# Twelve tiles of the imaginary hidden DFT move from the front of a DFT-attention kernel into its short attention sections, and most output projections move to the end

## The chip, the core and the metric

The kernel runs on one core of one Trainium2 chip. The metric is the device time of one execution in microseconds. A core has five engines with their own instruction streams: TensorE (PE), VectorE (DVE), ScalarE (ACT), GpSimd (POOL) and SyncE (SP, which here only issues DMAs). They are ordered against each other by semaphores alone.

## What is computed

For a sequence of 2048 tokens of width 512, a gate mixes two branches of the same input:

```
g = sigmoid((x * gate_w).sum(-1, keepdims=True))
a = x @ dft_hid_re.T ;  b = x @ dft_hid_im.T          # DFT along the hidden dimension
y = dft_seq_re @ a - dft_seq_im @ b                   # DFT along the sequence, real part
q, k, v = split_heads(x @ wqkv, 32 heads of 16)
o = softmax(q @ k.T * 16 ** -0.5) @ v                 # per head, then heads joined
out = g * y + (1 - g) * (o @ wo)
```

## The kernel before

**Precision.** Every float32 operand of the dense products is split into a high and a low fp32r part, and each product of two operands becomes three TensorE products (high-high, high-low, low-high). With four blocks of 128 along the hidden dimension, one 128x512 tile of `x @ W` takes 12 products of 512 columns. The value products of the attention are plain float32 (two TensorE instructions each).

**Front.** The q and k projections come first, then V (16 tiles of 12 products) and the imaginary hidden DFT `b` (16 tiles of 12). The first 8 V tiles are made with all 128 rows of the array. The other 8 and all 16 tiles of `b` go through `pairs_of` and `phase`: every product is cut into two row halves of 64, and two tiles run beside each other, one in each half. A phase has 24 such half products, and four phases make four tiles. Into them go the first score tiles for the row maxima (`a_tile`: one 128x512 score tile, reduced to its maxima by DVE, L296), `LEAD` = 57 key blocks for two heads each: alternately six and four tiles a phase. A tile of `b` is copied out of PSUM by ACT, split by POOL, and stored to DRAM (`b_done`, L370 to L373); for the first four tiles `b_done` also splits one block of the real DFT weight into SBUF (`wre`).

**Attention sections.** From then on TensorE works in sections that one string of slots each writes out by hand. A section belongs to one row half: the dense products of the DFT chain go into that half and score products into the other one, beside them. In a string, `a` is a score tile for a maximum (ended by a DVE reduce, 683 ns), `s` a score tile for an exponential (ended by an ACT activation, 628 ns); the digit is the PSUM bank; `-` is a dense product alone; a slot of two letters has no dense product but one score tile in each half; `|` are the value products of one unit. A unit is one key tile of one pair of heads for half of the queries: four exponentials fill its `pt` tile, then four value products add into the bank `acc`. Each section holds two units. Bank 6 is `acc` itself: between the copy that empties it at a section's start (`part`, ACT, L832) and the value products at the section's end it serves as a seventh bank for scores. Two sections, one for each half, make one chain of dense products.

There are three kinds. 13 pairs of short sections (THIN) hold the real hidden DFT, 12 products to a chain; ACT copies the finished tile out as `y` (L492) and POOL splits it back into `xab`. 96 pairs of FULL sections hold the sequence DFT, 16 products. 13 pairs of NINE sections hold output projections without their last block of heads, 9 products; their strings have the two units' value products apart. All maxima and exponentials come from two streams that the strings consume in order, so a string's letters also set which unit's exponentials are how far ahead of its value products.

**Tail.** The last 22 units have no maxima left. Scores, value products and the rest of the projections are interleaved by a loop over units (`sides`, `whole`), then the last head pair is finished (`LastPair`). SP's DMAs are issued in the order of the program, many of them by a table of due units (`at`, `run_plan`).

What orders the engines around a section's end: the first value product of a section overwrites `acc`, so it waits for the exponential that still reads a score in bank 6; and a unit's last value product waits for the last of the four exponentials that fill its `pt`.

Of the kernel before, what the change touches and what calls it, by code (L numbers as in the profile page):

```python
# [15 lines left out]
P = 128  # L16
# [8 lines left out]
LEAD = 57  # L25
# [6 lines left out]
def mix_kernel(ctx: ExitStack, tc: tile.TileContext, xa_t, xa, wqkv, w_hid, w_seq, wo, gate_w, out):  # L32
# [52 lines left out]
    oh_d = [[dram.tile([P, 2, S // 2], F32, name=f"oh{hf}{ct}") for ct in range(3)] for hf in range(2)]  # L85
# [29 lines left out]
    wv = [[const.tile([P, D], F32R, name=f"wv{v}{kt}", tag=f"w{4 * v + kt}") for kt in range(KT)] for v in range(2)]  # L115
    wch = st1.tile([P, KT, D], F32R, name="wch")
    wcl = st1.tile([P, KT, D], F32R, name="wcl")
# [77 lines left out]
    with tc.tile_pool(name="qk", bufs=1, reuse_waits="tile") as pool:  # L195
# [24 lines left out]
        for kt in range(KT):  # L220
            add(wch[:, kt], wcl[:, kt], w_hid[1, :, kt], nc.gpsimd)
# [145 lines left out]
    def b_done(s, ps):  # L367
# [6 lines left out]
        if s < KT:  # L374
            hi_lo(wre[0][s], wre[1][s], wrs.pop(0), nc.gpsimd)
# [42 lines left out]
    for s in range(8):  # L418
# [5 lines left out]
    pairs_of(range(8, NT), *wv, v_done)  # L424
# [5 lines left out]

    wre = [[const.tile([P, D], F32R, name=f"wre{v}{kt}", tag=f"w{4 * v + kt}") for kt in range(KT)] for v in range(2)]
    ab = [xab[s // 4][:, s % 4] for s in range(NT)]
    pairs_of(range(NT), *([w[:, kt] for kt in range(KT)] for w in (wch, wcl)), b_done)
# [46 lines left out]
    def real():  # L480

        for s, t in enumerate(ab):
            chain = Chain(*((psA, "a") if s in (0, 2) else (psD, "d")), 12)
            for kt in range(KT):
                h1, l1 = (t[:, v, kt * P:(kt + 1) * P] for v in range(2))
                yield chain, h1, wre[0][kt], None
                yield chain, h1, wre[1][kt], None
                yield chain, l1, wre[0][kt], partial(real_next, s, t, chain) if kt == KT - 1 else None

    def real_next(s, t, chain):  # L490
        y = work.tile([P, D], F32, name="y", bufs=2)
        nc.scalar.copy(y, chain.ps)  # L492
        psA.read(chain.ps)
# [123 lines left out]
    def block(step, hf, ct, half):  # L617

        if step == 0:
            t = work.tile([P, 2, D], F32, name="no")  # L620
            load_o(t[:, 0], t[:, 1], hf, ct, half * D)
# [11 lines left out]
    last_o = []  # L633

    def parts(hi, lo, src):
        nc.vector.tensor_copy(hi, src)
        nc.vector.tensor_tensor(lo, src, hi.bitcast(F32), ALU.subtract)

    def last_block(step, hf, n, eng):

        if step == 0:
            if not last_o:
                last_o.append(place(1, F32, "o_raw"))
            t = last_o[0][:, hf]
            load_o(t[:, 0], t[:, 1] if hf else None, hf, 3, 0, n)
        elif step == "sums":
            load_o(None, last_o[0][:, hf, 1], hf, 3, 0, n)
        elif step == 1:
            t = last_o[0][:, hf]
            eng.tensor_tensor(t[:, 0], t[:, 0], t[:, 1], ALU.mult)  # L650
        else:
            o = last_o[0][:, hf, 0]
            if hf:
                ts = [work.tile([P, 2, D], F32R, name=f"o_l{x}", tag=x) for x in ("no", "nh")]
                for i, t in enumerate(ts):
                    parts(t[:, 0], t[:, 1], o[:, i * D:(i + 1) * D])
                oh[hf, 3] = tiles(ts[0]) + tiles(ts[1])
            else:
                t = place(2, F32R, "o_l")[:, 0]
                parts(t[:, 0], t[:, 1], o)  # L660
                oh[hf, 3] = tiles(t)
# [31 lines left out]
    def load_yg(hf, ts):  # L693
# [5 lines left out]
        if not hf and ts[-1] == 7:  # L699
            for x, n in (("qs0", 4), ("ks0", 1)):  # L700
# [309 lines left out]
    def pairs():  # L1010

        for i in range(NT - 3):
            yield THIN, take(hid, 12)
# [132 lines left out]
```

## Time and profile before

| what | value |
|---|---|
| time, median of 3 runs | 1655.51 us (1655.06 to 1655.59) |
| span of the profiled execution, first to last instruction | 1653.7 us, 1.8 us under that median |
| TensorE, share of the span busy | 100%, granted clock 0.999 |
| DVE, ACT, POOL | 83%, 76%, 41% |
| V tiles with all rows, eight | 92.95 to 114.81 us |
| phases, 24 | 114.81 to 195.21 us |
| short sections, 26 | 208.26 to 347.08 us between value products |
| FULL sections, 192 | about 353 to 1449 us |
| NINE sections, 26 | to 1591 us |
| tail | 1591 to 1653.7 us |

The profile gives the span of its execution and no other time of it. Matmuls are pipelined and their ends are modelled, so two products of which each shows 390 ns can start 0.23 us apart, and a busy TensorE can still be waiting. The start times are what to read. Rows of a view by time merge equal instructions that follow each other: "x4" with 2.14 us means that four of them ended 2.14 us after the first began.

### The profile page before, as it was taken

To read this page: it belongs to the slowest core of one execution; us is meant where nothing else is said; L and a number is where in the kernel's file an instruction comes from. 1 tells how busy PE (TensorE), PEld (TensorE's weight loads), DVE (VectorE), ACT (ScalarE), POOL (GpSimd) and SP (SyncE) were. 2 spreads that over 40 slices of the span, in tenths; PEclk is the share of its full clock that TensorE was granted. 3 is DMA by queue.
4 is the path that set the end of the run, shared out by engine and by line. 5 is a ranking of instruction groups with operands and counts; after the bars stand their busy time and mean duration, and the time that the engine had idled before them with its cause. 6 is when DMAs were issued, how large, how long until landed. Compare 5 with 4: busy or idle time off the path is not lost.

```text
span 1653.7 us, 34501 instructions
## 1 busy us (share of the span) xinstructions
PE 1646.4 (100%) x13082; PEld 995.5 (60%) x13082; DVE 1372.1 (83%) x2338; ACT 1264.0 (76%) x2477; POOL 683.8 (41%) x651
## 2 busy tenths in 40 slices
PE   9999999999999999999999999999999999999998
PEld 7888966655555555555555555555555555544454
DVE  5439888888888888888888888888888888899954
ACT  5312289988888788887888878888788887889996
POOL 0204634443433456434343455544444455333330
PEclk9999999999999999999999999999999999999999
DMA  9977401314141534223147535224141536371014
GB/s 287 355 164 154 160 2 28 51 39 80 58 79 47 98 94 100 71 60 71 41 97 251 106 102 119 66 67 78 51 87 59 113 104 128 130 206 27 23 46 142
DMA packets 85247, 167.17 MB, mean 101 GB/s; under 512 B 22460, under 2 KB 22716, under 8 KB 81068
## 3 DMA queue, kind: packets, MB, share of 16 engines
q1 hardware_dynamic: 84648, 164.30, 39.0%
q8 instruction: 103, 1.69, 0.5%
q10 hardware_dynamic: 432, 0.66, 0.1%
q14 instruction: 64, 0.52, 0.1%
HBM read 109.67 MB, written 55.17 MB: 100 GB/s over the span
## 4 chain that ended last, share of the span: by engine, by line
PE 99%; DMA 0%; DVE 0%; DVEq 0%; ACT 0%; SPq 0%; issue 0%
PE acc L851 28%; PE a L294 23%; PE s L805 21%; PE d L476 9%; PE s L388 3%; PE acc L805 3%; PE acc L294 2%; PE s L422 1%; PE d L388 1%; PE acc L813 1%; PE a L111 1%; PE a L109 1%; PE s L111 1%; PE s L109 1%; PE a L110 1%; PE s L110 1%
## 5 line engine op out<-in xcount | busy, mean ns | idle before, releaser
L296 DVE TENSOR_REDUCE mx<-a 128x1 f32<-128x512 f32 x1828 | 1140.8, 683 | 164.0 <-PE a L294 103.1
L806 ACT ACTIVATE pt<-s 128x512 f32<-128x512 f32 x1792 | 946.4, 628 | 15.2 <-PE s L805 11.2
L294 PE MATMUL a<-ks,qs 64*128 64x512 f32 (+1 forms) x1828 | 677.3, 410 | 0.0
L476 PE MATMUL d<-xab,ch 64*128 64x512 f32 x2016 | 648.5, 396 | 0.0
L805 PE MATMUL s<-qs,ks 64*128 64x512 f32 (+1 forms) x1792 | 583.3, 397 | 0.0
L833 POOL TENSOR_TENSOR oe<-oe,part 128x512 f32<-128x512 f32 x215 | 278.1, 1293 | 653.9 <-ACT part L832 609.3
L851 PE MATMUL acc<-pt,vt 128*17 128x512 f32 x3968 | 479.0, 595 | 0.0
L294 PEld LDWEIGHTS a<-ks,qs 64*128 64x128 f32 (+1 forms) x1828 | 324.1, 184 | 244.6 <-issue 134.4
L476 PE MATMUL d<-xab,cl 64*128 64x512 f32 x1008 | 399.7, 397 | 0.0
L805 PEld LDWEIGHTS s<-qs,ks 64*128 64x128 f32 (+1 forms) x1792 | 321.9, 184 | 84.9 <-ACT pt L806 29.6
L476 PEld LDWEIGHTS d<-xab,ch 64*128 64x128 f32 x2016 | 366.5, 184 | 9.4
L832 ACT COPY part<-acc 128x512 f32<-128x512 f32 x215 | 126.2, 587 | 196.0 <-issue 174.1
L851 PEld LDWEIGHTS acc<-pt,vt 128*17 128x17 f32 x3968 | 89.0, 96 | 228.3 <-issue 148.4
L476 PEld LDWEIGHTS d<-xab,cl 64*128 64x128 f32 x1008 | 185.6, 184 | 5.0
L461 POOL TENSOR_TENSOR cl<-craw,ch 128x512 fp32r<-128x512 f32 x126 | 162.2, 1287 | 10.1
L296 DVE TENSOR_REDUCE mx<-acc 128x1 f32<-128x512 f32 x220 | 151.8, 690 | 12.2
L806 ACT ACTIVATE pt<-acc 128x512 f32<-128x512 f32 x244 | 148.7, 609 | 0.0
L805 PE MATMUL acc<-qs,ks 64*128 64x512 f32 (+1 forms) x244 | 95.5, 391 | 0.0
L294 PE MATMUL acc<-ks,qs 64*128 64x512 f32 (+1 forms) x220 | 85.8, 390 | 0.0
L460 POOL CAST ch<-craw 128x512 fp32r<-128x512 f32 x126 | 77.0, 611 | 18.8 <-PE d L476 13.1
L476 PE MATMUL d<-wre,xab 64*128 64x512 f32 x336 | 81.7, 388 | 0.0
L476 PE MATMUL d<-wo_hl,o_hl 64*128 64x512 f32 x252 | 66.7, 395 | 0.0
(178 smaller groups left out, 1232.5 us busy)
## 6 DMA issues: line engine op xcount, KB each, us to landing
craw<-w_seq SPq DMA_DIRECT2D x128, 256.0 KB
qk<-hl SPq DMA_DIRECT2D x32, 512.0 KB
qs<-qk SPq DMA_DIRECT2D x96, 128.0 KB
ks<-qk SPq DMA_DIRECT2D x96, 128.0 KB
b<-hl SPq DMA_DIRECT2D x16, 512.0 KB
xab<-b SPq DMA_DIRECT2D x16, 512.0 KB
o<-oe SPq DMA_DIRECT2D x62, 128.0 KB
oh<-nh SPq DMA_DIRECT2D x12, 512.0 KB
```

The costliest lines, as they stand in the source:

```text
L109: nc.tensor.matmul(ps, sh, mh, start=first, stop=False)
L294: nc.tensor.matmul(ps, qs[p % 2][r, qt * P:(qt + 1) * P], ks[p % 2][r, kb * 512:(kb + 1) * 512], start=True, stop=True)
L296: user = nc.vector.tensor_reduce(mx[p % 2][:, h, qt, kb:kb + 1], ps, AX.X, ALU.max)
L388: i = nc.tensor.matmul(ps, st[r], mv[r], start=not half and not j, stop=half == 1 and j == 11)
L460: nc.gpsimd.tensor_copy(h1, raw)
L461: nc.gpsimd.tensor_tensor(l1, raw, h1.bitcast(F32), ALU.subtract)
L476: i = nc.tensor.matmul(self.ps, st[r], mv[r], start=not self.begun, stop=stop)
L805: nc.tensor.matmul(ps, ks[p % 2][rr, kt * P:(kt + 1) * P], qs[p % 2][rr, q0:q0 + 512], start=True, stop=True)
L806: return nc.scalar.activation(pts[u][:, 2 * qb + h], ps, AF.Exp, bias=0.0, scale=DH ** -0.5)
L832: nc.scalar.copy(part[0], acc)
L833: nc.gpsimd.tensor_tensor(total, total, part[0], ALU.add)
L851: i = nc.tensor.matmul(acc[32 * j:32 * j + 17], v[:, 16 * h:16 * h + 17], pt[:, j], start=begin, stop=done or close)
```

## The change

Twelve of the 16 tiles of `b` leave the front. `LEAD` falls from 57 to 45 and the front now has 4 V tiles with all rows, then 12 V tiles and 4 tiles of `b` in 16 phases, with six maxima in every phase but the first. The 12 other tiles go through the same short sections as the real DFT, ahead of it, so there are 25 pairs of short sections in place of 13. Their string is new: it has 8 maxima and 8 exponentials in place of 7 and 8, and no slot with a dense product alone. The number of NINE pairs falls from 13 to 1, and the projections that were in them follow in the tail with all rows. The real DFT weight is split in the front, goes to DRAM (`wr_d`), and is loaded over the imaginary weight when the last tile of `b` has been made. The last block of heads goes through DRAM like the others (`block`, `load_last`).

```diff
-LEAD = 57
+LEAD = 45
+AHEAD = 4
...
-        (nc.vector.tensor_copy if s < 8 else nc.scalar.copy)(vt[:, s, :, 17:33], pv[:, :, 1])
+        (nc.vector.tensor_copy if s < AHEAD else nc.scalar.copy)(vt[:, s, :, 17:33], pv[:, :, 1])
...
-        if s < KT:
-            hi_lo(wre[0][s], wre[1][s], wrs.pop(0), nc.gpsimd)
+        wt = st1.tile([P, 2, D], F32R, name="hl", bufs=4)
+        hi_lo(wt[:, 0], wt[:, 1], wrs.pop(0), nc.gpsimd)
+        nc.sync.dma_start(wr_d[s], wt.bitcast(F32))
...
-            if maxima and j in ((2, 6, 10) if made % 2 else (3, 9)) and a_next < LEAD:
+            if maxima and j in (2, 6, 10) and a_next < LEAD:
...
-    for s in range(8):
+    for s in range(AHEAD):
...
-    pairs_of(range(8, NT), *wv, v_done)
+    pairs_of(range(AHEAD, NT), *wv, v_done)
...
-    pairs_of(range(NT), *([w[:, kt] for kt in range(KT)] for w in (wch, wcl)), b_done)
+    pairs_of(range(AHEAD), *wim, b_done)
...
+        for n, (c, s) in enumerate([(1, s) for s in range(AHEAD, NT)] + [(0, s) for s in range(NT)]):
+            t, w = ab[s], wim if c else wre
...
+    def hidden_next(c, s, t, chain, kt):
+        if c and s == NT - 1:
+            if not wre:
+                wre.extend(w_hidden("wre"))
+            for v in range(2):
+                nc.sync.dma_start(wre[v][kt].bitcast(F32), wr_d[kt][:, v])
+        if kt == KT - 1:
+            (imag_next if c else real_next)(s, t, chain)
+
+    def imag_next(s, t, chain):
+        y = work.tile([P, D], F32, name="y", bufs=2)
+        nc.scalar.copy(y, chain.ps)
+        psA.read(chain.ps)
+        hl = work.tile([P, 2, D], F32R, name="bhl", tag=("no", "nh")[s % 2])
+        nc.gpsimd.tensor_copy(hl[:, 0], y)
+        nc.gpsimd.tensor_tensor(hl[:, 1], y, hl[:, 0].bitcast(F32), ALU.subtract)
+        nc.sync.dma_start(b_d[s], hl.bitcast(F32))
...
-    THIN = ("a1S0 a2 a3 s5 s4 - a1 s0 s6 s5 s2 a3 a4 s0A1 | |",
-            "a1S0 a2 a3 s5 s4 - a1 s0 s6 s5 s2 a3 a4 s0A1 | |")
+    THIN = ("a5S2 a1 s0 s6 a3 s2 a5 s4 a1 s6 s0 a2 a3 a4S5 | |",) * 2
...
-        for i in range(NT - 3):
+        for i in range(2 * NT - AHEAD - 3):
             yield THIN, take(hid, 12)
         for i in range(2 * NT * 3):
             yield FULL, take(seq, 16)
-        for gen, n in ((proj(1, (0, 1, 2), one), 8), (first, 5)):
-            for i in range(n):
-                yield NINE, take(gen, 9)
+        yield NINE, take(first, 9)
...
-    def last_pair(fill):
+    def last_pair(before, fill):
         x = LastPair(1, [(psS, "s")])
         x.copy(4)
-        pump(fill, 2)
+        drain(before)
         x.turn()
-        pump(fill, 4)
+        pump(fill, 12)
         x.back()
+        pump(fill, 12)
+        x.products([(psA, "a")] * 3 + [(psD, "d")], (1, 2, 0, 3), (0,))
         drain(fill)
-        x.products([(psA, "a")] * 3 + [(psD, "d")], (1, 2, 0, 3), (0,))
...
-    whole = {506: (eighth, 3), 508: (last, 9), 510: (last, 12)}
+    begun = beside((of(first, 9), of(first, 9)), (of(first, 9), of(first, 9)), (of(third, 3), of(third, 3)))
+    whole = {506: (three_more, 3), 508: (three_more, 6), 510: (fourth, 12)}
...
-    last_pair(late)
+    run_plan(UNITS)
+    last_pair(fourth, proj(0, (0, 1, 2, 3), [(psS, "s")]))
```

The lines of the change's own functions below are those of the changed kernel: L301 is the score product of a maximum (L294 before), L808 that of an exponential (L805 before), L809 the exponential (L806), L854 the value product (L851), L835 the copy of `acc` to `part` (L832), L510 the copy of a finished tile to `y` (L492). "[waits ...]" names whose semaphores an instruction waits for.

ACT, one short section in which a tile is copied out, before: the copy of `acc`, eight exponentials of score tiles (`s`, and `acc` for bank 6) into `pt` tiles, and the copy to `y`.

```order
L832 COPY part_2448<-acc_208 128x512 [waits PE_49,Pool_49]
L806 ACTIVATE pt_3296<-s_3316 128x512 [waits PE_49]
L806 ACTIVATE pt_3247<-s_3328 128x512 [waits PE_49]
L806 ACTIVATE pt_3296<-s_3332 128x512 [waits PE_49]
L806 ACTIVATE pt_3296<-s_3341 128x512 [waits PE_49]
L806 ACTIVATE pt_3345<-acc_208 128x512 [waits PE_49,Activation_49]
L806 ACTIVATE pt_3345<-s_3349 128x512 [waits PE_49]
L806 ACTIVATE pt_3353<-s_3354 128x512 [waits PE_49,Activation_49]
L492 COPY y_3362<-d_3251 128x512 [waits PE_49]
L806 ACTIVATE pt_3353<-s_3369 128x512 [waits PE_49]
```

The same section in the changed kernel:

```order
L835 COPY part_2077<-acc_214 128x512 [waits PE_49,Pool_49]
L809 ACTIVATE pt_2827<-s_2828 128x512 [waits PE_49,Activation_49]
L809 ACTIVATE pt_2827<-s_2836 128x512 [waits PE_49]
L809 ACTIVATE pt_2827<-acc_214 128x512 [waits PE_49]
L809 ACTIVATE pt_2847<-s_2848 128x512 [waits PE_49]
L809 ACTIVATE pt_2847<-s_2856 128x512 [waits PE_49]
L809 ACTIVATE pt_2864<-acc_214 128x512 [waits PE_49]
L809 ACTIVATE pt_2864<-s_2868 128x512 [waits PE_49]
L510 COPY y_2876<-d_2761 128x512 [waits PE_49]
L809 ACTIVATE pt_2827<-s_2888 128x512 [waits PE_49]
```

The exponential that reads `acc` last has moved from the fifth place to the sixth. The eighth, behind the copy to `y`, now fills the last quarter of `pt_2827`; before, it filled a tile of the section that follows.

PE at the end of these two sections, before (the last score products and the value products of the units in `pt_3247` and `pt_3296`):

```order
L476 MATMUL d_3251<-wre03_1474,xab2_206 128x512
L294 MATMUL a_3366<-ks1_976,qs1_974 128x512 [waits Activation_49]
L805 MATMUL s_3369<-qs0_973,ks0_975 128x512 [waits Activation_49]
L294 MATMUL a_3372<-ks1_976,qs1_974 128x512 [waits DVE_49]
L851 MATMUL acc_208<-pt_3247,vt_972 17x512 [waits Activation_49]
L851 MATMUL acc_208<-pt_3247,vt_972 17x512 x3
L851 MATMUL acc_208<-pt_3296,vt_972 17x512 x4
```

And in the changed kernel (units in `pt_2757` and `pt_2827`):

```order
L482 MATMUL d_2761<-wim03_229,xab3_213 128x512
L301 MATMUL a_2882<-ks1_988,qs1_986 128x512 [waits DVE_49]
L301 MATMUL a_2885<-ks1_988,qs1_986 128x512 [waits Activation_49]
L808 MATMUL s_2888<-qs0_985,ks0_987 128x512 [waits DVE_49]
L854 MATMUL acc_214<-pt_2757,vt_984 17x512 [waits Activation_49]
L854 MATMUL acc_214<-pt_2757,vt_984 17x512 x3
L854 MATMUL acc_214<-pt_2827,vt_984 17x512 x3
L854 MATMUL acc_214<-pt_2827,vt_984 17x512 [waits Activation_49]
```

The first value product waits for ACT as before. The last one waits for ACT too, which it did not before. In the section between two of these, which has no copy to `y`, only the first value product waits.

ACT where the front ends and the sections begin, changed kernel: the copies of the last tiles of `b`, and between them the high parts (`hl`) of the real DFT weight's blocks, each of which needs a buffer whose last content a DMA has taken to DRAM.

```order
L377 COPY b_1763<-s_1633 128x512 [waits PE_49]
L107 CAST hl_1768<-raw_1244 128x512 [waits DMAHW6_49,DMAHW5_49,Pool_49]
L377 COPY b_1773<-d_1634 128x512 [waits PE_49]
L107 CAST hl_1778<-raw_1379 128x512 [waits DMAHW7_49,DMAHW2_49,Pool_49]
L377 COPY b_1824<-s_1635 128x512 [waits PE_49,Activation_49,Pool_49]
L107 CAST hl_1829<-raw_1430 128x512 [waits DMAHW1_49,DMAHW0_49,Pool_49]
L377 COPY b_1834<-s_1636 128x512 [waits PE_49,Activation_49,Pool_49]
L107 CAST hl_1839<-raw_1581 128x512 [waits DMAHW3_49,DMAHW2_49,Pool_49]
L783 ACTIVATE ng_199<-z_197 128x16 [waits DVE_49]
L510 COPY y_1867<-a_1854 128x512 [waits PE_49]
L809 ACTIVATE pt_1873<-s_1874 128x512 [waits PE_49]
```

Before, the copies of the last tiles of `b` stood there one after another, with the weight's blocks 12 tiles earlier.

More of the change, by code (lines that the diff above doesn't have):

```diff
@@ L631, in block, with load_last @@
             nc.sync.dma_start(oh_d[hf][ct][:, :, half * D:(half + 1) * D], hl.bitcast(F32))
[L633 to L661, printed above, removed]
+    def load_last(hf):
+        t = main.tile([P, 2, 2 * D], F32R, name=f"o_l{hf}", tag="qs0" if hf else "ks0")
+        nc.sync.dma_start(t.bitcast(F32), oh_d[hf][3])
+        oh[hf, 3] = tiles(t)
     few = work.tile([P, D], F32, name="few")
@@ L699, in load_yg @@
         if not hf and ts[-1] == 7:
[L700 to L702 removed]
+            for first in (3, 7):
+                y4 = work.tile([P, 4, D], F32, name="pt", bufs=4)
+                yp.update({first + j: y4[:, j] for j in range(min(4, 8 - first))})
         for t in ts:
@@ L901, in mix_kernel @@
                         at(last + du + 8 * half, block, step, hf, ct, half)
+            else:
+                for half in range(2):
+                    for step, du in enumerate((6, 8, 8)):
+                        at(last + du + (2 if hf == 0 else 0) + (4 if hf else 2) * half, block, step, hf, ct, half, n)
+                at(494 if hf else 511, load_last, hf)
     for p in range(2, NP):
@@ L1045, in mix_kernel @@
     assert not any(a_left.values())
-    third = proj(1, (3,), side, range(7))
-    eighth = proj(1, (3,), two, (7,))
-    last = proj(0, (3,), three[1:] + three[:1], range(7))
-    early, late = proj(0, (0,), side[1:], (7,)), proj(0, (1, 2, 3), [(psS, "s")], (7,))
+    third = proj(1, (3,), side, range(2))
+    three_more = proj(1, (3,), two, range(2, 5))
+    fourth = proj(1, (0, 1, 2, 3), three, range(5, 8))
     def behind(i, other):
```

52 lines of the change are left out of this document (21 added, 31 removed).

## The prediction

> **What bounds the kernel now.** I read the page's shares and chain first, then the stages by time, then single sections on each engine.
>
> ```profile
> PE 1646.4 (100%) x13082; PEld 995.5 (60%) x13082; DVE 1372.1 (83%) x2338; ACT 1264.0 (76%) x2477; POOL 683.8 (41%) x651
> PE 99%; DMA 0%; DVE 0%; DVEq 0%; ACT 0%; SPq 0%; issue 0%
> ```
>
> The whole chain lies on TensorE, so the change has to be priced by start times of TensorE, stage by stage. The view by windows has whole V tiles, phases, short sections, NINE sections and tail as the rows shown; the columns are the stretch, its length, then each engine's busy time.
>
> ```profile
> core 0: us, PE busy (x) PEld busy (x) DVE busy (x) ACT busy (x) POOL busy (x), PEclk, DMA share, GB/s
> 92.95:114.81 21.86, 21.86 (x99) 17.84 (x97) 4.27 (x10) 3.90 (x9) 1.34 (x2) 1.00 0.89 163
> 114.81:195.21 80.40, 80.40 (x692) 71.99 (x691) 71.77 (x117) 16.67 (x38) 34.51 (x37) 1.00 0.55 147
> ...
> 208.26:347.08 138.82, 138.82 (x1119) 85.75 (x1118) 114.28 (x189) 124.98 (x246) 57.56 (x58) 1.00 0.18 29
> ...
> 1455.46:1584.43 128.97, 128.97 (x986) 62.08 (x984) 120.64 (x200) 117.47 (x229) 45.48 (x42) 1.00 0.26 66
> 1590.85:1653.70 62.85, 57.00 (x423) 30.06 (x419) 25.19 (x45) 46.22 (x95) 10.07 (x12) 0.97 0.33 101
> ```
>
> A short section takes 138.82 / 26 = 5.34 us. ACT is busy 125 of 139 us there, so I look at how the two engines interlock. First TensorE, two sections: first product, value products, next first product.
>
> ```profile
> 300.90 0.49 PE L294 MATMUL a<-ks,qs 64*128 64x512 f32 x1
> ...
> 304.39 1.91 PE L851 MATMUL acc<-pt,vt 128*17 128x512 f32 x16
> 306.23 0.50 PE L294 MATMUL a<-ks,qs 64*128 64x512 f32 x1
> 306.57 0.39 PE L294 MATMUL a<-ks,qs 64*128 64x512 f32 x1
> 306.80 0.39 PE L294 MATMUL a<-ks,qs 64*128 64x512 f32 x1
> ...
> 309.73 1.91 PE L851 MATMUL acc<-pt,vt 128*17 128x512 f32 x16
> ```
>
> With T for the first product (300.90), the value products start at T + 3.49, and the next section 1.84 us behind them. Inside, a slot starts every 0.23 us after a first one of 0.34. ACT in the same two sections, and DVE in the second:
>
> ```profile
> 301.09 0.59 ACT L832 COPY part<-acc 128x512 f32<-128x512 f32 x1 [0.75 <-PE acc L851]
> 301.57 2.14 ACT L806 ACTIVATE pt<-s 128x512 f32<-128x512 f32 x4
> 303.58 0.62 ACT L806 ACTIVATE pt<-acc 128x512 f32<-128x512 f32 x1
> 304.06 1.12 ACT L806 ACTIVATE pt<-s 128x512 f32<-128x512 f32 x2
> 305.01 0.65 ACT L492 COPY y<-d 128x512 f32<-128x512 f32 x1
> 305.48 0.68 ACT L806 ACTIVATE pt<-s 128x512 f32<-128x512 f32 x1
> ...
> 308.92 0.62 ACT L806 ACTIVATE pt<-acc 128x512 f32<-128x512 f32 x1
> 309.40 1.61 ACT L806 ACTIVATE pt<-s 128x512 f32<-128x512 f32 x3
> 306.76 4.45 DVE L296 TENSOR_REDUCE mx<-a 128x1 f32<-128x512 f32 x7 [0.89 <-PE s L805]
> ```
>
> ACT cannot begin before the section's first products exist: its copy starts at T + 0.19, its first exponential at T + 0.67, and from there it runs without a gap. The fifth exponential, which reads `acc`, ends at 303.58 + 0.62, T + 3.30, and the value products that overwrite `acc` start 0.19 us later. The view of waits in this stage:
>
> ```profile
> PEld acc L851 <- ACT pt L806: 6.1, 25, 0.2
> ```
>
> In 25 of the 26 sections the value products waited for ACT (6.1 us in all). So a short section is already set by ACT's fifth exponential, as much as by its 14 slots. The sixth, of 0.62 us, ends at T + 3.78 (304.06; 309.40 in the second section gives T + 3.79); the eighth, behind the copy to `y`, at T + 5.26 (305.48 + 0.68).
>
> **The change, part by part.**
>
> *Short sections.* ACT's work in a section stays the same: copy, eight exponentials, and in every second one a copy to `y`. Only its order against the value products moves. In the new string bank 6 is used twice, and its last exponential is the sixth. So the first value product waits until T + 3.79, not 3.30. It follows at once at best and 0.19 us later at worst (as above), so the next section starts at T + 5.63 to 5.82; I take 5.72. In the section that copies a tile out, the last value product also waits for the eighth exponential, at T + 5.26. That product's two passes run alone after it. A unit by itself takes 0.98 us to the next first product:
>
> ```profile
> 1573.69 1.05 PE L851 MATMUL acc<-pt,vt 128*17 128x512 f32 x8
> ...
> 1579.29 1.05 PE L851 MATMUL acc<-pt,vt 128*17 128x512 f32 x8
> 1580.27 0.50 PE L476 MATMUL d<-wo_hl,o_hl 64*128 64x512 f32 x1
> ...
> 1584.43 1.05 PE L851 MATMUL acc<-pt,vt 128*17 128x512 f32 x8
> ```
>
> So that section lasts 5.26 + 0.98 = 6.24, or 6.43 with 0.19 between; I take 6.33. A pair is 12.05 us (11.87 to 12.25), where it was 10.68. Everything behind the waiting product on TensorE waits too: the next section's scores, hence both DVE and ACT. DVE has eight reduces 0.63 us apart ((4.45 - 0.68) / 6), 5.0 us, and is covered. TensorE's own 14 slots also wait for banks; the last such wait, at slot 13 for the bank that the fifth exponential frees at T + 3.30, leaves 0.34 us for that slot and some 0.1 to the value products, T + 3.75, and is covered by the sixth exponential. 25 pairs of 12.05 are 301.3, against 138.8 before: **+162.5 us**.
>
> The Trainium skill says in "TensorEngine Tiling (Array Packing)", section PSUM Bottleneck, that tiling speeds up TensorE but not the evacuation of PSUM, which may become the bottleneck. The trace agrees: the value products start 0.19 us behind ACT's fifth exponential. By TensorE's slots alone a pair would take no more than now, and 25 pairs 267 us.
>
> *NINE sections.* A pair takes 1584.43 - 1573.69 = 10.74 us, and 12 pairs go: **-128.9**.
>
> *Front.* Four whole V tiles go (21.86 / 8 = 2.73 each, -10.9), as they become pairs. Of the phases:
>
> ```profile
> 95.67 12.63 PE L422 MATMUL s<-wv,xab 128*128 128x512 f32 x55
> ...
> 172.62 1.89 DVE L296 TENSOR_REDUCE mx<-a 128x1 f32<-128x512 f32 x3
> ```
>
> A phase with six maxima has 12 + 3 slots of 0.23, 3.45 us on TensorE, but 6 x 0.605 = 3.63 on DVE ((1.89 - 0.68) / 2 from start to start). Before, phases of six and four alternated, 80.40 / 24 = 3.35 us each, and DVE caught up. Now DVE sets every one: 2.8 + 15 x 3.63 + 0.4 for the maxima's own reductions = 57.7, against 80.4. Front: **-33.7**; -36 if TensorE set it, -32 with more gaps.
>
> *START.* Of `b` only four tiles remain, two in each of the last two phases, and each now costs POOL three instructions up to the end:
>
> ```profile
> 152.18 0.61 POOL L371 CAST hl<-b 128x512 fp32r<-128x512 f32 x1 [11.65 <-issue]
> ...
> 155.37 0.62 POOL L371 CAST hl<-b 128x512 fp32r<-128x512 f32 x1
> 193.48 1.29 POOL L372 TENSOR_TENSOR hl<-b,hl 128x512 fp32r<-128x512 f32 x1
> DMA  0000009999999899999000000799979999899720
> 198.27 0.59 ACT L492 COPY y<-a 128x512 f32<-128x512 f32 x1 [0.82 <-PE a L476]
> ```
>
> One tile takes 155.37 - 152.18 = 3.19 us on POOL. The DMA row covers 195 to 199 us in slices of 0.1: a tile that POOL finished at 194.77 had left SBUF at 196.9, 2.2 us later. ACT's cast for the fourth weight block needs the buffer of the second, which POOL finishes two tiles (6.4, and 0.8 to begin) after the last phase but one, and a DMA empties 2.2 us later. Cast and gate behind it put the copy to `y` at 10.1, against 3.65 + 3.06 (198.27 - 195.21) = 6.7 before: 3.4 us late, and the first exponential with it. TensorE needs the copied bank a little later: **+2.7** (0 to 6).
>
> *Weight reload.* Eight DMAs of 256 KB on SP each follow the last read of their block, and have a section to land: nothing, at most 2. The 12 tiles' stores (512 KB each on SP) and POOL's two instructions for each (0.62 + 1.29) have a pair of 12 us to lie in: nothing.
>
> *Tail.* 108 products go whole to the end, at (12.63 - 0.39) / 54 = 0.227 us: +24.5. Nothing covers them. The end itself gets shorter: now 6.2 us lie between the last product and the end, through ACT, POOL and a DMA.
>
> ```profile
> 1647.46 0.40 PE L758 MATMUL a<-w,o 32*128 32x512 f32 x2
> 1649.24 0.74 DVE L675 SCALAR_TENSOR_TENSOR yp<-d,omg,yp 128x512 f32<-128x512 f32 x1
> ```
>
> After a last projection come 0.4, a DVE combine of 0.75, and the 3.7 us from 1649.98 to the end, 1.3 less. Tail: **+23.2** (22 to 25).
>
> Sum: 162.5 - 128.9 - 33.7 + 2.7 + 23.2 = **+25.8 us**, a span of 1679.5. The span lies 1.8 us under the median of the runs, so **1681 us**. With the lower ends (11.87 a pair, -36, 0, +22) it is +15, with the upper ones (12.25, -32, 6 + 2, +25) +40; ends do not all fall together, so the likeliest case's own range is 1674 to 1691.
>
> **Rivals.** *Short sections stay with TensorE* (ends on the other side). If the exponentials came early enough, a pair would take 10.68 as now, also 14 slots a section. 25 are 267, and the sum is 128.2 - 128.9 - 33.7 + 2.7 + 23.2 = -8.5: 1647 us. For it speaks that the new string has one score in each half at both ends and no lone dense product, so no slot is lost. Against it speaks the wait row above, and that ACT starts from each section's own first products. It decides where a pair stays under 12.05 - 25.8 / 25 = 11.0 us. "TensorEngine Tiling (Array Packing)" of the Trainium skill, section Theoretical Speedup, gives up to twice for 64 rows; by that rule this rival would hold, and the trace agrees only while PSUM is emptied in time.
>
> *Only the sixth exponential's wait shows.* Should the wait for the eighth fall beside other work, pairs take 2 x 5.72 = 11.44, 15 us less than my sum: 1666. Against it: nothing else follows on TensorE than the next section.
>
> *The banks cost more than the exponentials.* Waits at slots 9 to 13 could push the sixth score itself, and each 0.2 us a section costs 10: 1691 or more. For it: the new string refills nine banks within 3 us.
>
> **How the numbers follow.** Values wait as read, 0.75; banks cost more, 0.08; only the sixth, 0.06; TensorE keeps the sections, 0.11. The prediction is the first, 1681. The range of 1665 to 1694 takes in the third and most of the second, and leaves out the gain. Slower by over 0.2%, about what a measurement of this kernel can tell from no change, holds in the first three: 0.87 with sizes allowed for; faster 0.11; within 0.2% 0.02.
>
> **What would show it.** Short sections alternate, about 5.7 and 6.3 us from value products to value products, ACT without gaps in them and TensorE waiting for `pt`. 15 phases of about 3.6 us. A copy to `y` in START that comes late. About 25 us more from the tail's start to the end. I am wrong if short sections come near 5.3 us, or if the front gives more than 36 us.

## The result, and the profile after

The changed kernel takes 1713.83 us (median of 4 runs, 1712.43 to 1714.62), the kernel before 1655.38: a ratio of 1.0353, 95% interval 1.0339 to 1.0368. The forecast was 1681, with 1665 to 1694 as its range. So the sign was right and the size was not: the profiled span grew by 58.3 us (1653.7 to 1712.0), where the sum gave 25.8.

The page's totals and the engines of its chain, after:

```profile
PE 1674.0 (98%) x13022; PEld 1003.6 (59%) x13022; DVE 1361.7 (80%) x2328; ACT 1253.5 (73%) x2469; POOL 676.0 (39%) x650
PE 94%; DMA 3%; POOL 1%; SPq 1%; DVE 0%; issue 0%; ACT 0%; POOLq 0%
```

TensorE had 99% of the chain before and has 94% now. The other 6% is DMA, POOL and SP: stretches in which something else than TensorE's own order set the time. Where they lie is seen in the view by windows, stage by stage (stretch, length, busy time of PE, PEld, DVE, ACT and POOL, granted clock, DMA share, GB/s). After: whole V tiles, phases, START, short sections, FULL, the one pair of NINE, and the tail in two pieces:

```profile
93.15:104.25 11.10, 11.10 (x49) 8.83 (x47) 2.57 (x6) 1.74 (x4) 0.59 (x1) 1.00 0.78 158
104.25:168.19 63.94, 59.25 (x476) 51.34 (x475) 53.26 (x91) 11.85 (x33) 8.36 (x9) 0.95 0.61 114
168.19:188.99 20.80, 17.00 (x74) 11.34 (x73) 10.92 (x18) 9.21 (x19) 13.31 (x14) 0.84 0.58 231
188.99:484.51 295.52, 295.08 (x2202) 157.68 (x2201) 245.17 (x413) 237.89 (x475) 108.39 (x109) 1.00 0.25 55
484.51:1586.91 1102.40, 1102.40 (x9218) 642.77 (x9216) 973.18 (x1663) 898.99 (x1761) 508.69 (x474) 1.00 0.36 88
1586.91:1599.32 12.41, 12.41 (x94) 5.41 (x92) 8.71 (x15) 10.92 (x22) 4.75 (x5) 1.00 1.02 408
1599.32:1640.08 40.76, 16.44 (x101) 8.30 (x97) 0.37 (x2) 12.90 (x27) 10.02 (x13) 0.67 0.36 118
1640.08:1712.00 71.92, 68.29 (x432) 42.59 (x431) 21.41 (x36) 33.34 (x70) 9.15 (x10) 1.00 0.40 133
```

And the rows of before that the prediction did not show, START, FULL and the same two pieces of the tail, cut at the third value products behind its start:

```profile
195.21:208.26 13.05, 13.05 (x74) 9.85 (x73) 8.40 (x16) 8.08 (x17) 8.84 (x10) 1.00 0.41 162
347.08:1449.45 1102.37, 1102.37 (x9217) 637.69 (x9216) 972.60 (x1663) 899.35 (x1762) 508.85 (x473) 1.00 0.38 90
...
1590.85:1604.45 13.60, 13.60 (x101) 7.98 (x97) 2.98 (x8) 12.80 (x27) 4.83 (x6) 1.00 0.05 14
1604.45:1653.70 49.25, 43.40 (x324) 22.08 (x323) 22.21 (x38) 33.42 (x70) 5.23 (x6) 0.96 0.40 125
```

| stage | before | after | change | forecast |
|---|---|---|---|---|
| up to the first V tile | 92.95 | 93.15 | +0.2 | 0 |
| whole V tiles and phases | 102.26 | 75.04 | -27.2 | -33.7 |
| START | 13.05 | 20.80 | +7.8 | +2.7 |
| short sections (26, now 50) | 138.82 | 295.52 | +156.7 | +162.5 |
| FULL | 1102.37 | 1102.40 | 0 | 0 |
| NINE (13 pairs, now 1; from 1449.45 to 1590.85 before) | 141.40 | 12.41 | -129.0 | -128.9 |
| tail | 62.85 | 112.68 | +49.8 | +23.2 |
| sum | | | +58.3 | +25.8 |

Of the 32.5 us between forecast and measurement, 26.6 lie in the tail, 6.7 in the front, 5.1 in START; 5.8 go the other way in the short sections. In the tail the first piece is the odd one: 101 products on TensorE before and after, 13.60 us before, 40.76 after. Its TensorE in the order of time:

```profile
1606.94 0.65 PE L808 MATMUL s<-qs,ks 64*128 64x512 f32 x4
1631.91 0.79 PE L482 MATMUL a<-wo_hl,o_hl 64*128 64x512 f32 x1 [24.32 <-POOL tick L1067]
...
1633.92 3.61 PE L854 MATMUL acc<-pt,vt 128*17 128x512 f32 x16
```

TensorE stood still for 24.3 us, and the row names a one-element memset on POOL: `tick`, with which `side_by_side` keeps the two turns of a pair of chains apart. Sixteen value products behind it took 3.61 us instead of 1.91, at a granted clock of 0.67 over the piece. POOL's own rows say what `tick` stood behind. L651 is the multiply of `block(1, 3)`, the last block of heads for the second half of the queries, called the last tile below; it is made in two halves of 512 queries.

```profile
1612.65 1.26 POOL L651 TENSOR_TENSOR no<-no 128x512 f32<-128x512 f32 x1 [16.54 <-DMA no<-r]
...
1618.59 0.22 POOL L323 TENSOR_TENSOR nhl<-nm,nhl 128x16 fp32r<-128x16 f32 x1
...
1628.55 1.26 POOL L651 TENSOR_TENSOR no<-no 128x512 f32<-128x512 f32 x1 [8.82 <-DMA m<-mt]
...
1631.76 0.10 POOL L1067 MEMSET tick<- 128x1 f32 x1
```

POOL waited 16.5 us at the multiply (L651) of the last tile's first half for the reciprocal rows `r`, and later 8.8 us at that of the second half. The rows were stored into a full house: in the 12.41 us between the end of FULL and the tail the DMA engines were busy at a share of 1.02, at 408 GB/s. Before, 13 pairs of NINE lay at that place, with a share of 0.26. What the end of the sequence DFT sets free (the `o_hl` loads, the gated sums) had 141 us to arrive in and now has 12.

### The profile page after: what moved, and what is told of

It reads as the page before. It is cut to its first block, busy times and chain, and to the rows that moved or that the text cites. A ratio compares the mean times of both kernels' runs of the same rounds, so it can differ in the third digit from the quotient of the medians.

```text
span 1712.0 us, 34331 instructions
## 1 busy us (share of the span) xinstructions
PE 1674.0 (98%) x13022; PEld 1003.6 (59%) x13022; DVE 1361.7 (80%) x2328; ACT 1253.5 (73%) x2469; POOL 676.0 (39%) x650
## 4 chain that ended last, share of the span: by engine, by line
PE 94%; DMA 3%; POOL 1%; SPq 1%; DVE 0%; issue 0%; ACT 0%; POOLq 0%
PE acc L854 27%; PE a L301 22%; PE s L808 18%; PE d L482 11%; PE acc L808 3%; PE acc L301 2%; PE s L396 2%; PE s L482 2%; PE acc L816 1%; DMA ks<-qk 1%; PE a L112 1%; PE a L111 1%; PE s L112 1%; PE s L111 1%; PE a L113 1%; PE s L113 1%
## 5 line engine op out<-in xcount | busy, mean ns | idle before, releaser
L809 ACT ACTIVATE pt<-s 128x512 f32<-128x512 f32 x1742 | 928.6, 630 | 35.8 <-PE s L808 30.9
L301 PE MATMUL a<-ks,qs 64*128 64x512 f32 (+1 forms) x1834 | 690.3, 408 | 7.3 <-DMA ks<-qk 4.7
L808 PE MATMUL s<-qs,ks 64*128 64x512 f32 (+1 forms) x1742 | 591.5, 400 | 1.2 <-ACT b L377 1.2
L301 PEld LDWEIGHTS a<-ks,qs 64*128 64x128 f32 (+1 forms) x1834 | 330.4, 184 | 275.4 <-issue 158.2
L854 PE MATMUL acc<-pt,vt 128*17 128x512 f32 x3968 | 490.9, 597 | 0.0
L808 PEld LDWEIGHTS s<-qs,ks 64*128 64x128 f32 (+1 forms) x1742 | 317.9, 185 | 59.9 <-ACT pt L809 9.3
L835 ACT COPY part<-acc 128x512 f32<-128x512 f32 x215 | 126.3, 587 | 230.7 <-issue 174.6
L854 PEld LDWEIGHTS acc<-pt,vt 128*17 128x17 f32 x3968 | 94.2, 96 | 247.6 <-issue 155.8
L809 ACT ACTIVATE pt<-acc 128x512 f32<-128x512 f32 x294 | 180.6, 614 | 0.3 <-PE acc L808 0.3
L303 DVE TENSOR_REDUCE mx<-acc 128x1 f32<-128x512 f32 x214 | 148.1, 692 | 11.2
L808 PE MATMUL acc<-qs,ks 64*128 64x512 f32 (+1 forms) x294 | 122.1, 415 | 0.0
L482 PE MATMUL d<-wre,xab 64*128 64x512 f32 x384 | 95.6, 393 | 0.4 <-DMA wre<-wr 0.3
L301 PE MATMUL acc<-ks,qs 64*128 64x512 f32 (+1 forms) x214 | 83.7, 391 | 0.0
L482 PEld LDWEIGHTS d<-wre,xab 64*128 64x128 f32 x384 | 69.0, 184 | 3.5 <-DMA wre<-wr 1.9
```

The lines of the kernel that those rows point to most:

```text
L301: nc.tensor.matmul(ps, qs[p % 2][r, qt * P:(qt + 1) * P], ks[p % 2][r, kb * 512:(kb + 1) * 512], start=True, stop=True)
L303: user = nc.vector.tensor_reduce(mx[p % 2][:, h, qt, kb:kb + 1], ps, AX.X, ALU.max)
L482: i = nc.tensor.matmul(self.ps, st[r], mv[r], start=not self.begun, stop=stop)
L808: nc.tensor.matmul(ps, ks[p % 2][rr, kt * P:(kt + 1) * P], qs[p % 2][rr, q0:q0 + 512], start=True, stop=True)
L809: return nc.scalar.activation(pts[u][:, 2 * qb + h], ps, AF.Exp, bias=0.0, scale=DH ** -0.5)
L835: nc.scalar.copy(part[0], acc)
```

## The experiments

Each was timed in three rounds beside the kernel before. Ratios are to that kernel on the same chip; the changed kernel's is 1.0353, and one thousandth is 1.66 us.

**e1: the tick on DVE.**

```diff
-        clock = nc.vector if u == 498 else nc.gpsimd
+        clock = nc.vector
```

> The changed kernel with one edit in the tail: the small memset that separates the two turns of a side-by-side group of projections (tick) is always DVE's, where two of the three were POOL's. Theory A (POOL's queue: the tick stood behind the last tile's multiply, cast and subtract, which wait for its transfers): the wait of 24.3 us and the slow clock behind it (6.16 instead of 4.43 us in the next section) go, but the last tile's products, 27 us earlier now, find their data still on the way: SP issues that load at 1635, TensorE would be there at 1628.6, so 9 to 10 us come back. About 1697 us. Theory B (TensorE would have waited for that data in any case, the tick is only the last to arrive): within 2 us of the changed kernel, 1714. Theory C (nothing else is late): 27 us less, 1687.

Measured: 1712.38 us, 1.0341 (1.0326 to 1.0357), nothing gained. Theory A's number is wrong and B's is right, but not for B's reason. TensorE in the tail, then DVE:

```profile
1621.01 0.79 PE L482 MATMUL a<-wo_hl,o_hl 64*128 64x512 f32 x1 [11.60 <-DVE tick L1067]
...
1632.76 1.43 PE L808 MATMUL s<-qs,ks 64*128 64x512 f32 x2 [7.34 <-DMA qs<-m]
```

```profile
1620.72 0.21 DVE L327 STREAM_TRANSPOSE mt<-nhl 128x32 f32<-128x32 f32 x1 [19.69 <-POOL nhl L323]
1620.88 0.06 DVE L1067 MEMSET tick<- 128x1 f32 x1
```

The tick now stood on DVE behind a transpose that waits for POOL's `nhl`, and `nhl` stands on POOL behind the same multiply. With that wait halved, the next came: scores needed the last pair's rows of maxima (`qs<-m`), which had left late by the same chain. One late multiply had three waiters, so moving one of them away from POOL bought nothing.

**e5 and e6: order of POOL and SP in the tail.** e5 moves the last tile's block in the plan; e6 does that and takes two loads out of SP's way.

```diff
-                    for step, du in enumerate((6, 8, 8)):
-                        at(last + du + (2 if hf == 0 else 0) + (4 if hf else 2) * half, block, step, hf, ct, half, n)
-                at(494 if hf else 511, load_last, hf)
+                    for step, du in enumerate((6, 10, 10) if hf else (8, 10, 10)):
+                        at(last + du + (6 if hf else 2) * half, block, step, hf, ct, half, n)
+                at(498 if hf else 511, load_last, hf)
```
```diff
-                load_yg(1, range(8, 14) if s // 4 == 2 else range(14, 16))
+                load_yg(1, range(8, 14)) if s // 4 == 2 else None
...
+    at(500, load_yg, 1, range(14, 16))
```

> The changed kernel with other places for the last tile's block in the plan of the tail: its first half's multiply, cast and subtract stand one unit pair later on POOL, behind the two small operations (nhl) that make the last pair's rows of maxima, the second half's loads on SP stand behind the transfer of those rows, and its multiply behind the first tick. Theory A (three waiters stood behind one multiply on POOL: the tick, the last rows of maxima, and through SP's queue the second half): the multiply still starts when its transfer lands, 1612.6, the tick follows at about 1617 in place of 1631.8, 14 to 15 us less: 1699. The rest of the stall stays, since SP's transfers start no earlier. Theory B (transfers alone set it, whatever POOL's order): within 2 us of 1714, as with the tick on DVE.

> As e5, and on SP the two last loads of the gated sums (yp<-yg of tiles 14 and 15), which wait for a store, no longer stand ahead of the last tile's reciprocal rows: they come after the tail has begun. Theory A: the rows leave SP about 5 us earlier, the first multiply starts at about 1607 and the first tick comes at 1611, so some 4 us of the 24.3 remain: 1692 to 1694. Theory B: no change to e5.

Measured: e5 1705.46 us, 1.0307 (1.0291 to 1.0322); e6 1702.18 us, 1.0286 (1.0270 to 1.0301). POOL's order is worth 8 us, half of what A gave, and SP's some 3 more. The first tick's wait fell from 24.3 us to 9.7 in e5, the 14 to 15 us that A named, and to 8.5 in e6. Part of that gain was lost at the second half, which now comes later, so that TensorE waits twice more (e6):

```profile
1616.31 0.79 PE L482 MATMUL a<-wo_hl,o_hl 64*128 64x512 f32 x1 [8.48 <-POOL tick L1068]
...
1634.17 0.49 PE L482 MATMUL a<-wo_hl,o_hl 64*128 64x512 f32 x1 [1.69 <-POOL tick L1068]
1644.10 0.46 PE L482 MATMUL d<-wo_hl,o_l 64*128 64x512 f32 x1 [2.03 <-DMA o_l<-oh]
```

Why the earlier rows helped so little is in SP's rows, the changed kernel first, then e6:

```profile
1597.87 1.22 SPq L622 DMA_DIRECT2D r<-rc  x2
...
1603.89 0.51 SPq L639 DMA_DIRECT2D no<-r  x1
```

```profile
1593.40 1.52 SPq L622 DMA_DIRECT2D r<-rc  x2
...
1603.30 0.51 SPq L639 DMA_DIRECT2D no<-r  x1
```

The first load of `r` waits until the rows have landed. They left SP 4.5 us earlier in e6, and that load came 0.6 us earlier. So the queue's order was only part of it; the transfers themselves were slow there, at a DMA share of 1.05 in e6 from 1593 to 1599 us.

**e9: the last tile without its rows.** The multiply by the reciprocal rows and the rows' loads are left out for the last tile, in both its halves (12 of its 24 loads). The expectation calls this tile the last head pair's first half.

```diff
-            load_o(t[:, 0], t[:, 1], hf, ct, half * D, n)
+            load_o(t[:, 0], t[:, 1] if (hf, ct) != (1, 3) else None, hf, ct, half * D, n)
...
-            nc.gpsimd.tensor_tensor(t[:, 0], t[:, 0], t[:, 1], ALU.mult)
+            if (hf, ct) != (1, 3):
+                nc.gpsimd.tensor_tensor(t[:, 0], t[:, 0], t[:, 1], ALU.mult)
```

> As e6, but for the last head pair's first half the reciprocal rows are not loaded and the multiply by them is left out (12 of its 24 loads and two POOL instructions; that tile is not normalised). Theory A (what is left of the stall in e6, 8.5, 1.7 and 2.0 us at the ticks and at o_l, is this tile's chain of transfers, rows out, rows in, 12 loads a half, so close behind the end of the sequence DFT): the first half is ready at about 1608, the first tick passes at once, and with the slow clock behind it 11 to 14 us go: 1688 to 1691. The tail then takes about 23 us more than before's 62.85, as its 108 products alone give. Theory B (the tail is longer for another reason, the products' own order or DVE's combines): 1698 or more.

Measured: 1691.02 us, 1.0214 (1.0197 to 1.0231), 12 us below e6, as A said. The edit takes away the rows' landing, the multiply and half of the loads at once, so it prices this tile's path and none of the three alone. No wait for a tick is left, and the tail's row is

```profile
1597.43:1687.60 90.17, 84.00 (x531) 51.47 (x527) 21.78 (x37) 46.34 (x95) 15.84 (x20) 0.97 0.46 155
```

90.2 against 62.85 before: 27.3 more. One section in it still takes 8.56 us instead of 4.43, where scores wait 2.0 us for `qs<-m` and run at a slower clock behind that; without those 4.1 it is 23.2, which is what 108 products and the shorter end were priced at.

**e2 and e3: the short sections' string.** e2 lets the last slot's two products change halves; e3 is a string written anew, with the same eight maxima and eight exponentials.

```diff
-a5S2 a1 s0 s6 a3 s2 a5 s4 a1 s6 s0 a2 a3 a4S5 | |
+a5S2 a1 s0 s6 a3 s2 a5 s4 a1 s6 s0 a2 a3 s5A4 | |      (e2)
+s5A2 a4 s3 a0 s6 a5 s1 s2 s4 a6 s3 a1 a5 s0A2 | |      (e3)
```

> The changed kernel with one edit in the string of the short sections: the last slot's two products change their halves of TensorE (a4S5 becomes s5A4), so the eighth exponential is of a unit that this section doesn't use. Theory: every second section loses its wait for the eighth exponential and takes 5.6 us as the others do; a pair 11.2 instead of 11.80, 25 pairs 15 us less: 1699. Rival (the alternate section is long because of the copy to y or the banks): no change, 1714.

> The changed kernel with the short sections' string written anew, with the same eight maxima, eight exponentials and twelve projected products a section: acc is read by the third exponential and by a maximum (a6) in place of the sixth exponential, and the last unit's product changes its half as in e2. Theory (the order of the readers of banks sets the sections, not the number of products): worked out by hand from the rows' pitches (ACT 0.48, DVE 0.605, slots 0.23), a section 5.5 us, a pair 11.0 against 11.80: 20 us less, 1694. Rival (DVE's eight maxima set it once ACT does not): a pair no better than e2's 11.2, 1699 or more.

Measured: e2 1701.35 us, 1.0276 (1.0258 to 1.0295), 12.7 us less; e3 1702.74 us, 1.0284 (1.0267 to 1.0302). In e2 every section takes 5.62 us; the alternation is gone, so the long section was the wait for the eighth exponential:

```profile
250.80 1.91 PE L854 MATMUL acc<-pt,vt 128*17 128x512 f32 x16
256.42 1.91 PE L854 MATMUL acc<-pt,vt 128*17 128x512 f32 x16
```

e3's theory missed, and the number of its rival (DVE's maxima set it) held: the values no longer wait for an exponential, and a section still took 5.6 us. From the first product to the value products TensorE needs 3.77 us (251.97 to 255.74), where the string of before needs 3.49: small waits along the string put back what the one wait had cost. The last reader of bank 6 is now a maximum, and the view of waits from 200 to 480 us shows the values waiting for it in 48 of some 50 sections:

```profile
PEld acc L854 <- DVE mx L303: 14.7, 48, 0.4
```

In the section that starts at 251.97 this maximum ended on DVE at 255.62, 0.12 us ahead of the values. But TensorE's last slot there also starts late, 3.44 us into the section (255.41), where in the kernel before it starts 3.08 us in (252.84 to 255.92); which of the two holds the section was not settled.

**e4: the new string in the kernel before.** Only the string of the 26 short sections is exchanged.

> The kernel before with one part of the change alone: its 26 short sections run the changed kernel's string (eight maxima in place of seven, the new order). Theory: a pair takes 11.80 instead of 10.68, 13 pairs 14.6 us more; the 26 maxima done early leave gaps in the last sections that save at most 3 us: 1667 to 1670. Rival (the short sections got longer in the changed kernel through the stores and loads of the 12 moved tiles): about 1655.

Measured: 1776.46 us, 1.0728 (1.0712 to 1.0744), 121 us more than before. Neither theory gave that. The sections themselves behave as forecast, in pairs of 11.80 (one from the middle):

```profile
261.13 1.91 PE L851 MATMUL acc<-pt,vt 128*17 128x512 f32 x16
266.75 2.50 PE L851 MATMUL acc<-pt,vt 128*17 128x512 f32 x16
272.93 0.62 PE L851 MATMUL acc<-pt,vt 128*17 128x512 f32 x4
```

5.62 and 6.18 us: the string alone, without the 12 moved tiles, makes the sections long. Of the other hundred, 64 us stand in one row of the view of waits, TensorE's for the stacks (14 times):

```profile
PE a L294 <- DMA ks<-qk: 63.6, 14, 6.4
```

The 26 maxima done early would bring the maxima of the next head pairs ahead of their stacks' loads; this reading was not tested, and where the rest went was not followed. So this kernel answers the question on the sections, by its rows, and not by its time; and its time warns that maxima cannot be moved ahead freely.

**e7, e8, e11: front and START.** e7 issues the four loads of the output weights behind the fills of the stacks:

```diff
-    wos = [staged(wo[:, kt]) for kt in range(KT)]
...
         nc.sync.dma_start(z_d[:, tb * 2 * D:(tb + 1) * 2 * D], zeros)
+    wos = [staged(wo[:, kt]) for kt in range(KT)]
```

e8 gives the stored pairs (`hl`) `bufs=6` instead of 4 at their five places. e11 moves the casts of the real weight blocks from `b_done` into `v_done`:

```diff
+        if s in range(9, 17, 2):
             wt = st1.tile([P, 2, D], F32R, name="hl", bufs=4)
             hi_lo(wt[:, 0], wt[:, 1], wrs.pop(0), nc.gpsimd)
-        nc.sync.dma_start(wr_d[s], wt.bitcast(F32))
+            nc.sync.dma_start(wr_d[(s - 9) // 2], wt.bitcast(F32))
```

> The changed kernel with the four loads of the output weights (wo, 1 MB) issued behind the small fills of the stacks instead of ahead of them. Theory A (the first maxima's wait of 4.7 us is for stack loads that share the DMA engines with these 1 MB): the stacks land 2 to 3 us earlier, the phases get that much shorter, 1711. Theory B (the stacks' own 1.5 MB set it, through 16 partitions at a time): no change, 1714.

> The changed kernel with six buffers instead of four for the pairs of tiles that are stored (hl). Theory A (ACT's weight casts wait there for a buffer, 3.2 and 1.8 us, and the first copy to y and the first exponential behind them): START is 3 to 5 us shorter, 1709 to 1711. Theory B (POOL's queue of casts and subtracts sets the copy in any case): 1 us or less, 1713 to 1714.

> The changed kernel with the four casts of the real weight blocks (hi_lo for wr, one ACT cast and one POOL subtract each, and their stores) moved out of the last phases into the V phases, one for every second V tile from the ninth on. Theory A (START is long because ACT's casts wait there for buffers and POOL, and the copy to y and the first exponential stand behind them, with a slower clock after each wait): the copy to y comes about 3.1 to 3.6 us after START begins, as before, in place of 7.5, and START takes 13 to 15 us in place of 20.8: 1707 to 1709. Theory B (POOL's splitting of the four tiles of b sets it whatever the weights do): START 18 us or more, 1711 to 1714.

Measured: e7 1715.05 us, 1.0393 (1.0335 to 1.0450), span 1713.0, no gain (one of its four runs took 1732.17, which widens the interval). The first maxima still wait 4.62 us, against 4.69: the output weights are not what the stacks wait for. e8 1711.75 us, 1.0342 (1.0326 to 1.0357), 2 us less by the medians, with intervals that overlap; its START takes 17.29 us (168.00 to 185.29) and the first copy to `y` comes at 172.62. e11 1721.10 us, 1.0398 (1.0381 to 1.0415), slower. Its two stages apart, phases and START:

```profile
104.05:182.13 78.08, 61.57 (x475) 53.62 (x475) 54.08 (x92) 13.05 (x35) 13.18 (x14) 0.87 0.57 121
182.13:195.18 13.05, 13.05 (x74) 9.81 (x73) 9.49 (x17) 8.08 (x17) 8.60 (x9) 1.00 0.52 207
```

START is back at 13.05 us, to the hundredth what it was before, so the weight casts and their stores were all of START's growth. The phases paid: 78.1 us against 63.9. The fourth cast waited on ACT, 14.2 us, for a load that SP had issued behind the next pair's stacks, and DVE's transpose for `nhl` behind it on POOL; TensorE stood still for 12.0 us (`a` at 172.22, for `mx`). The same pattern as in the tail, made by my own edit.

**e10: e2, e6 and e8 together.**

> The changed kernel with the edits of e2 (halves of the last slot), e6 (both parts of the tail) and e8 (six buffers) together. If they lie in different stages, their gains add: 12.5 + 11.6 + 2.1 less than 1713.8, 1687 to 1688, still slower than the kernel before. If the earlier start of the tail or another wait takes some back: 1690 or more.

Measured: 1688.71 us, 1.0197 (1.0181 to 1.0212). The parts lie in different stages and add, as expected. No version of the change tried here beats the kernel before.

## Why the prediction was wrong in size

*Tail, the step that failed.* The prediction said: "108 products go whole to the end [...] +24.5. Nothing covers them", and stopped at TensorE's products. That part held: from the third value products on the tail is 71.92 - 49.25 = 22.7 us longer, for a forecast of 23.2. What failed is that the tail's +23.2 put the last tile's path at nothing, and that "12 pairs go: -128.9" was priced as time alone. It cost 40.76 - 13.60 = 27.2 us, in two ways.

The first is cover. The row of NINE before, with its DMA share of 0.26, was quoted for its length and its last columns were not read. Before, the transfers that the end of the sequence DFT sets free filled the DMA engines from 1450 to 1465 us (share 0.92 to 1.04), 114 us ahead of the last tile's rows. Now the rows are stored into them, and wait on SP behind them. The second is the path itself. I had costed POOL and SP for the moved tiles in the short sections, and not for the last tile's block, whose multiply, cast, subtract, store and loads the diff puts into the tail's plan as well. SP's rows show both, before (the store of the rows and their last load) and after (the last load of each half):

```profile
1579.38 1.21 SPq L596 DMA_DIRECT2D r<-rc  x2
...
1590.49 0.59 SPq L613 DMA_DIRECT2D o_raw<-r  x1
```

```profile
1610.13 0.59 SPq L639 DMA_DIRECT2D no<-r  x1
...
1626.15 0.59 SPq L639 DMA_DIRECT2D no<-r  x1
```

Before, the rows were stored 11.5 us ahead of the tail and the last load left SP as the tail began (1590.85). After, they were stored 1.5 us ahead (1597.87, tail from 1599.32), and the first half's last load left 10.8 us into the tail, 11.2 later than before: I read that as the burst's share. The second half's last load left 16.0 us later still, and not for the burst, which was over (share 0.09 from 1602 to 1605 us). Before, 12 loads in one round served both halves; now there are 24 in two rounds, with the same 0.63 us from one issue to the next, and the second round stands on SP behind the store of the first half, which waits for POOL. e5 agrees: with the second half out of the first tick's way on POOL, the wait there fell by 14.6 us, and the 9.7 that stayed are the first half's. e5, e6 and e9 together took 23 us off the changed kernel, and 4.1 stayed in e9. No run put the cover back, so the split into 11 and 16 us is read from these rows and was not tested.

*Front.* "DVE sets every one" held (12 maxima take 7.17 us on DVE, the period of two phases), but the sum began with the first maxima at once. They waited for their stacks:

```profile
107.82 0.40 PE L301 MATMUL a<-ks,qs 48*128 48x512 f32 x1
112.91 0.76 PE L301 MATMUL a<-ks,qs 48*128 48x512 f32 x1 [4.69 <-DMA ks<-qk]
```

The stacks were on their way since 95 us. Before, eight whole V tiles lay over that, until 114.81; now four, until 104.25. I took 10.9 us for the four removed tiles and did not ask what they covered. The wait of 4.69 us and a slower clock behind it (0.95 over the phases) are most of the 6.7 us. e7 shows that the output weights' loads are not the reason; which of the transfers to the stacks lands last was not settled.

*START.* The step was right and its size too small. ACT waited as described, 3.19 us for a buffer and 1.79 for POOL:

```profile
172.15 0.62 ACT L107 CAST hl<-raw 128x512 fp32r<-128x512 f32 x1 [3.19 <-DMA wr<-hl]
...
175.05 0.62 ACT L107 CAST hl<-raw 128x512 fp32r<-128x512 f32 x1 [1.79 <-POOL hl L108]
...
175.69 0.57 ACT L510 COPY y<-a 128x512 f32<-128x512 f32 x1
```

The copy came 7.50 us into START against 3.06 before, 4.4 late where 3.4 was forecast. Of the 7.8 us that START grew by, TensorE stood idle for 3.8 (20.80 - 17.00), and its products took 3.9 more (17.00 - 13.05), at a granted clock of 0.84.

*Short sections.* Right in mechanism, 0.23 us a pair too dear. The second of two sections after, TensorE and then ACT:

```profile
255.31 0.50 PE L301 MATMUL a<-ks,qs 64*128 64x512 f32 x1
...
259.09 2.50 PE L854 MATMUL acc<-pt,vt 128*17 128x512 f32 x16
261.52 0.50 PE L301 MATMUL a<-ks,qs 64*128 64x512 f32 x1
```

```profile
258.39 0.65 ACT L809 ACTIVATE pt<-acc 128x512 f32<-128x512 f32 x1
258.86 0.67 ACT L809 ACTIVATE pt<-s 128x512 f32<-128x512 f32 x1
259.34 0.67 ACT L510 COPY y<-d 128x512 f32<-128x512 f32 x1
259.81 0.70 ACT L809 ACTIVATE pt<-s 128x512 f32<-128x512 f32 x1
```

The values start 0.05 us behind the sixth exponential (258.39 + 0.65 = 259.04), where I took 0.1, and that exponential ends at T + 3.73 instead of 3.79. Their burst lasts 2.50 instead of 1.91: it waits for the eighth, which ends at 260.51, and the next section starts 1.01 us behind that. The forecast's 0.98 for this was read from a unit of eight passes and used for the two that were left; why two take as long was not followed, so that its size came out right is in part luck. 5.6 and 6.2 alternate as written. 25 pairs at 11.82 make 295.5.

*Rivals.* "TensorE keeps the sections" is refuted by these rows. Its break-even of 11.0 us a pair was reached by no string tried: e2 came to 11.24, and 25 such pairs are 281 us, more than the 138.8 of the old short sections and the 129.0 of NINE together. With the other stages as measured it would lie lower, at 11.82 - 58.3 / 25 = 9.5. "Only the sixth exponential's wait" is what e2 made true by hand. "The banks cost more" was not what put the time over the range, though in e3 the waits along the string, for DVE's maxima among them, kept a section at 5.6 once the exponentials did not.

## What to carry to other kernels

When work is taken out between two stages, ask of every transfer that starts at the end of the first what it now lands behind: read the DMA share of the stage that goes, not only its length. When a step is moved in a plan, list for each engine and queue what stands behind its first waiting instruction; a one-element memset on an otherwise idle engine held TensorE for 24 us, and moving the memset alone did not help, since two more waiters stood behind the same multiply. Count a moved step's loads too, and what stands ahead of them on the issuing queue: twelve loads at 0.63 us each are 7.6 us on SP, even when the DMA engines are nearly idle. And before maxima or other look-ahead work is moved earlier, check what loads its inputs and when.

## What the runs showed of the hardware

A wait on TensorE was paid for a second time in clock: after the 24.3 us the products came 0.42 us apart instead of 0.23, and value products took 3.61 us instead of 1.91. The Trainium skill, "TensorE: Matmul & The Clock Gate", Part 1, says that the array falls to half rate after an idle window of about 3.4 us; that agrees here, with a granted clock of 0.50 from 1632 to 1636 us. But shorter waits were enough in START, which I had not expected: after two of 1.20 and 1.80 us (ending at 173.30 and 176.31), none as long as the page's window, the granted clock read 0.50 from 177 us on, and the 12 products of the second chain there took 4.06 us where those of the first took 3.01. In e9 one wait of 2.02 us for `qs<-m` was followed by a granted clock of 0.50 too (1612 to 1614).

Two small transfers of rows needed 4.8 us from the end of their issue to the next load's start in the changed kernel, and 8.4 us in e6, where they were issued into a stretch with a DMA share of 1.05.
